# Attention scores of two heads on the two row halves of TensorE, in three float32r passes, with keys and queries split once per pair of heads

## The chip, the cores and the metric

The kernel runs on one core of one Trainium2 chip. The metric is the device time of one execution in microseconds (us): the median of three runs. The profile is of one execution that took 1009.93 us on the device; its span, from the first to the last instruction, is 1008.2 us.

## The reference

Attention over 4 batches and 12 heads, sequence 448, head size 64, with a mixing of heads before and after the softmax ("talking heads"), then a two-layer perceptron:

```python
scores = scale * np.matmul(q, k.transpose(0, 1, 3, 2))          # per head, 448 x 448, scale 1/8
scores = np.einsum('bhij,hg->bgij', scores, w_pre)              # mix heads
scores = scores - np.max(scores, axis=-1, keepdims=True)
attn = np.exp(scores)
attn = attn / (np.sum(attn, axis=-1, keepdims=True) + 1e-09)
attn = np.einsum('bhij,hg->bgij', attn, w_post)                 # mix heads
x = np.matmul(attn, v)                                          # then (b i) x (h d) = 1792 x 768
h = x @ w_in                                                    # 768 x 2048
out = np.maximum(0.01 * h, h) @ w_out                           # 2048 x 768
```

All inputs and the output are float32.

## The kernel before

A *chunk* is 120 rows of the queries of one batch (88 in the last of the four chunks of a batch); there are 16 chunks. A chunk is cut into groups of ten rows: 12 groups (9 in the short chunk), dealt into three supergroups `s`. The main loop runs over chunks `n` and, inside a chunk, over 12 steps `t = 4 s + c`.

In a step of chunk `n` the program writes down, in this order: `softmax` of one group of the next supergroup (one float32 product with the block-diagonal `kpre` on TensorE into bank `psm`, a maximum on VectorE, an exponential on ScalarE; at a supergroup's last group also the reciprocals and the scaled matrix `kp` on VectorE); in steps 0 to 3 `scores` of three heads of chunk `n + 1`; then, one step late, `mix` of column block `c` of the supergroup before (products with `kp` into bank `psa`, copied to `at` or `half`) or, for c = 3, `values` of the chunk before (bank `psx`, copied to `xo`) around the mix; then `regroup`, a DMA that deals the scores `st` of chunk `n + 1` into group tiles `rt`; and in step 6 `prep_q` of chunk `n + 2`.

`mix` of the last column block writes its two 64-partition output halves as two matmuls (120x64 weights), and `values` writes the even and the odd head of a pair into output partitions 0 to 63 and 64 to 127, also as two matmuls (128x64 weights). These are halves of the array by column.

`scores` of one head are two float32r matmuls with all 128 rows: the keys lie in SBUF with their high part (rounded to float32r) in partitions 0 to 63 and their low part (the rest) in partitions 64 to 127; the queries lie twice, once in each half, and come as a low part `qlo` and a high part `qhi`. So the launch code hands over `q` and `k` doubled to 128 partitions. `prep_k` (lines 163 to 168) makes one head's keys: a cast of 128x448 on VectorE (L166) and a subtraction of 64x448 on GpSimd (L167). `prep_q` (lines 178 to 192) makes one chunk's queries in two calls each of a cast of 128x720 on ScalarE (L190) and a subtraction of 128x720 on GpSimd (L191). The banks `pss` are copied to `st` by ScalarE (L218) and, every third head, VectorE (L216).

GpSimd has one more job: two float32 operations of 128x384 (L116, L117), 60 times over the loop, at the end of the conversion of the perceptron's float64 weights (`Narrow`: ScalarE L99 and L100, VectorE L106, L109 and L112, then GpSimd).

Before the loop stands a prologue: the loads of the first chunk's queries and of 12 heads of keys, their split, the scores of chunk 0, the regrouping and four softmax groups. Behind the loop, from 528 us, runs the perceptron: only float32r matmuls of 128x448 in three passes (L368).

What sets the order: all of attention's matmuls are kept in program order on TensorE (`mm`, L153 and L154), and so are the pieces of `Narrow` on their engines. Everything else is ordered by a planner that puts an instruction on its engine's queue as early as its inputs and a free buffer allow in the planner's own timeline; each engine then works through its queue in that order. PSUM has eight banks: 2 `psm`, 2 `psa`, 1 `psx`, 3 `pss`.

## Time and profile before

| | |
|---|---|
| median of three runs | 1010.64 us (1010.62 to 1011.05) |
| profiled execution | 1009.93 us; span 1008.2 us |
| TensorE busy, share of the span | 947.7 us, 94% |
| VectorE busy | 705.8 us, 70% |
| ScalarE busy | 399.9 us, 40% |
| GpSimd busy | 250.9 us, 25% |
| DMA | 170.98 MB, mean 170 GB/s |
| mean granted TensorE clock | 0.981 |

TensorE's busy time is modelled and matmuls are pipelined, so a busy TensorE may still be waiting a little at each matmul; its idle time is more telling. Names in a row are those of the program (`pss` is a scores bank, `qlo` the low part of the queries). PE is TensorE's matmuls, PEld its weight loads, DVE VectorE, ACT ScalarE, POOL GpSimd, SP the engine that issues most DMAs.

### The profile page before, as it was taken

To read this page: it belongs to the slowest core of one execution; us is meant where nothing else is said; L and a number is where in the kernel's file an instruction comes from. 1 tells how busy PE (TensorE), PEld (TensorE's weight loads), DVE (VectorE), ACT (ScalarE), POOL (GpSimd) and SP (SyncE) were. 2 spreads that over 40 slices of the span, in tenths; PEclk is the share of its full clock that TensorE was granted. 3 is DMA by queue.
4 is the path that set the end of the run, shared out by engine and by line. 5 is a ranking of instruction groups with operands and counts; after the bars stand their busy time and mean duration, and the time that the engine had idled before them with its cause. 6 is when DMAs were issued, how large, how long until landed. Compare 5 with 4: busy or idle time off the path is not lost.

```text
span 1008.2 us, 16745 instructions
## 1 busy us (share of the span) xinstructions
PE 947.7 (94%) x6192; PEld 803.9 (80%) x6192; DVE 705.8 (70%) x1248; ACT 399.9 (40%) x891; POOL 250.9 (25%) x213
## 2 busy tenths in 40 slices
PE   4889899998999989999899999999999999999998
PEld 2567678776777767777679999999999999999997
DVE  6588987789787897778785656865557555665553
ACT  4566566565666656666541112311113111211111
POOL 5146743358434574344120001100000000000000
PEclk9999999998999989999989999999999999999999
DMA  5876756856568654686554434553336333353331
GB/s 179 277 214 224 225 188 202 252 211 214 189 205 267 217 175 154 208 259 222 182 164 142 138 109 139 165 166 110 109 110 199 112 104 111 108 164 110 110 94 55
DMA packets 102917, 170.98 MB, mean 170 GB/s; under 512 B 30260, under 2 KB 76852, under 8 KB 102836
## 3 DMA queue, kind: packets, MB, share of 16 engines
q1 hardware_dynamic: 101108, 167.16, 53.0%
q10 hardware_dynamic: 1728, 2.75, 0.7%
q8 instruction: 49, 0.80, 0.3%
q14 instruction: 32, 0.26, 0.1%
HBM read 107.75 MB, written 23.59 MB: 130 GB/s over the span
## 4 chain that ended last, share of the span: by engine, by line
PE 81%; DVE 9%; issue 4%; DMA 2%; ACT 2%; SPq 1%; POOL 0%; DVEq 0%; ACTq 0%; POOLq 0%
PE psh L368 23%; PE pso L368 23%; PE psa L154 12%; PE psm L154 11%; PE psx L154 6%; PE pss L154 6%; DVE kst L166 2%; DVE kp L255 1%; ACT et L242 1%; DVE stat L241 1%; SPq L228 1%; DVE top L109 1%; DVE top L106 1%; DMA rt<-st 1%; DVE at L290 1%
## 5 line engine op out<-in xcount | busy, mean ns | idle before, releaser
L154 PEld LDWEIGHTS psa<-kp,et 120*128 120x128 f32 (+2 forms) x1800 | 175.0, 176 | 67.0 <-issue 48.4
L154 PE MATMUL psm<-rt,kpre 120*120 120x448 f32 x360 | 180.9, 587 | 22.5 <-ACT et L242 18.9
L154 PE MATMUL psa<-kp,et 120*128 120x120 f32 (+2 forms) x1800 | 182.4, 262 | 20.0 <-DVE kp L255 14.3
L361 DVE CAST wh<-wr 128x768 fp32r<-128x768 f32 x128 | 72.9, 570 | 170.1 <-PE psh L368 113.0
L379 ACT ACTIVATE t<-psh 128x448 f32<-128x448 f32 x64 | 35.0, 547 | 312.2 <-PE psh L368 294.5
L242 ACT ACTIVATE et<-psm,stat 120x448 f32<-120x448 f32 x180 | 113.9, 633 | 86.4 <-DVE stat L241 83.5
L368 PE MATMUL psh<-xh,wl 128*128 128x448 f32 x384 | 140.7, 367 | 0.9 <-issue 0.9
L368 PE MATMUL pso<-gl,wh 128*128 128x448 f32 x384 | 140.2, 365 | 0.0
L368 PE MATMUL pso<-gh,wh 128*128 128x448 f32 x384 | 140.2, 365 | 0.0
L368 PE MATMUL psh<-xh,wh 128*128 128x448 f32 x384 | 140.2, 365 | 0.0
L368 PE MATMUL psh<-xl,wh 128*128 128x448 f32 x384 | 140.2, 365 | 0.0
L368 PE MATMUL pso<-gh,wl 128*128 128x448 f32 x384 | 139.1, 365 | 0.0
L241 DVE TENSOR_REDUCE stat<-psm 120x1 f32<-120x448 f32 x180 | 111.3, 618 | 35.1 <-PE psm L154 32.1
L362 DVE TENSOR_TENSOR wl<-wr,wh 128x768 fp32r<-128x768 f32 x128 | 122.9, 960 | 2.0
L116 POOL TENSOR_TENSOR w<-w,exp 128x384 f32<-128x384 f32 x60 | 62.8, 1046 | 217.0 <-DVE exp L112 91.7
L154 PE MATMUL pss<-kst,qlo 128*120 128x448 f32 (+1 forms) x192 | 94.3, 491 | 12.6 <-POOL kst L167 10.0
L218 ACT ACTIVATE st<-pss 120x448 f32<-120x448 f32 (+1 forms) x132 | 69.3, 543 | 65.4 <-PE pss L154 63.0
L154 PEld LDWEIGHTS psm<-rt,kpre 120*120 120x120 f32 x360 | 54.9, 193 | 36.7 <-ACT et L242 26.1
L368 PEld LDWEIGHTS psh<-xh,wl 128*128 128x128 f32 x384 | 72.1, 188 | 7.1 <-issue 1.0
L290 DVE COPY at<-psa 128x480 f32<-128x480 f32 (+2 forms) x112 | 68.6, 613 | 13.1 <-PE psa L154 11.8
L368 PEld LDWEIGHTS pso<-gh,wh 128*128 128x128 f32 x384 | 72.2, 188 | 5.7
L368 PEld LDWEIGHTS pso<-gl,wh 128*128 128x128 f32 x384 | 72.1, 188 | 5.7
(59 smaller groups left out, 1345.8 us busy)
## 6 DMA issues: line engine op xcount, KB each, us to landing
wr<-w_dram SPq DMA_DIRECT2D x126, 384.0 KB
rt<-st SPq DMA_DIRECT2D x176, 210.0 KB
craw<-in_w_moe SPq DMA_DIRECT2D x64, 384.0 KB
w_dram<-w SPq DMA_DIRECT2D x60, 192.0 KB
kraw<-in_k SPq DMA_DIRECT2D x48, 224.0 KB
qraw<-in_q SPq DMA_DIRECT2D x11, 720.0 KB
xr<-x_dram SPq DMA_DIRECT2D x24, 224.0 KB
vt<-in_v SPq DMA_DIRECT2D x12, 384.0 KB
```

The costliest lines, as they stand in the source:

```text
L106: pin(nc.vector.tensor_scalar(top, z.bitcast(U32), 3, 0x7FFFFFF8, op0=ALU.logical_shift_left, op1=ALU.bitwise_and))
L116: pin(nc.gpsimd.tensor_mul(w, w, self.exp.bitcast(F32)))
L154: tc.keep_in_program_order(nc.tensor.matmul(*args, **kw))
L166: hi(t, raw)
L218: nc.scalar.activation(s_t[n][:m, h, :], ps[:m, :S], AF.Copy, scale=scale)
L241: nc.vector.tensor_reduce(st[:kk, 0, g:g + 1], ps[:kk, :S], axis=AX.X, op=ALU.max, negate=True)
L242: nc.scalar.activation(e[:kk], ps[:kk, :S], AF.Exp, bias=st[:kk, 0, g:g + 1], accum_out=st[:kk, 1, g:g + 1])
L290: copy(at[:, :, i:i + full * ROWS].rearrange("p h (g r) -> p g h r", r=ROWS), ps[:, :w * full].rearrange("p (g h r) -> p g h r", h=nh, r=R ...
L361: nc.vector.tensor_copy(hi, raw)
L362: nc.vector.tensor_sub(lo, raw, hi.bitcast(F32))
L368: nc.tensor.matmul(ps, w[a][:, c * P:(c + 1) * P], x[e], start=first and j == 0, stop=last and j == 2)
L379: nc.scalar.activation(t, ps[:, :S], AF.Copy, scale=0.01)
```

## The change

Keys and queries are no longer doubled in SBUF: partitions 0 to 63 hold the even head of a pair, partitions 64 to 127 the odd one. (The launch code is as before; the loads take the half that they need.) `prep_k` splits a pair at once into a high tile and a low tile of 128x448, the subtraction on VectorE. `prep_q` splits six pairs in two calls of 128x360 (three pairs each), cast on ScalarE, subtraction on VectorE. GpSimd does neither any more.

`scores(n, j)` does two pairs (four heads): per pair three passes (low queries with high keys, high with low, high with high), each pass two matmuls with 64 rows, one per head, on the two row halves and into two banks. The product of the two low parts is dropped. Four banks are filled: two `pss` and two `psx` (now two of these, and two `pss` in place of three). Three of the four are copied by ScalarE, one by VectorE.

The three calls of a chunk stand in steps 2, 6 and 10, and two of them lie a chunk earlier than before: in step 2 of chunk `n` the last third of chunk `n + 1`, in steps 6 and 10 the first two thirds of chunk `n + 2`. So `st` has two buffers, `prep_q` moves to step 3, the load of queries to step 6 and one chunk ahead, and `regroup` runs from step 4 to 8 (before from 3 to 7). Keys of the next batch are loaded and split every second step over some 17 steps. The prologue does the first two thirds of chunk 1's scores as well.

```diff
@@ -141,54 +141,58 @@
     pool = pools(psum, "left")
     ps_m = pool("ps_m", 2, space=PSUM)
     ps_a = pool("ps_a", 2, space=PSUM)
-    ps_x = pool("ps_x", 1, space=PSUM)
+    ps_x = pool("ps_x", 2, space=PSUM)
     pool = pools(right, "right")
     p_raw = pool("raw", 1)
     p_q = pool("q", 1)
-    p_k = pool("k", H + 2)
-    p_s = pool("s", 1)
+    p_k = pool("k", NPAIR)
+    p_s = pool("s", 2)
     p_c = pool("c", 1)
-    ps_s = pool("ps_s", 3, space=PSUM)
+    ps_s = pool("ps_s", 2, space=PSUM)
 
     def mm(*args, **kw):
         tc.keep_in_program_order(nc.tensor.matmul(*args, **kw))
 
     kw_t, k_t, q_t, v_t, s_t, r_t, e_t, kp_t, at_t, xo_t = ({} for _ in range(10))
 
-    def load_k(b, h):
+    def load_k(b, a):
         t = p_raw.tile([P, S], F32, tag="k", name="kraw", bufs=6)
-        kw_t[b, h] = t
-        return nc.sync.dma_start(t, k[b, :, h, :])
-
-    def prep_k(b, h, hi=nc.vector.tensor_copy, lo=nc.gpsimd.tensor_sub):
-        raw = kw_t.pop((b, h))
-        t = p_k.tile([P, S], F32R, tag="k", name="kst")
-        hi(t, raw)
-        lo(t[D:], raw[D:], t[D:].bitcast(F32))
-        k_t[b, h] = t
-
-    def load_q(n, *heads):
+        kw_t[b, a] = t
+        for e in range(2):
+            up = slice(D * e, D * (e + 1))
+            nc.sync.dma_start(t[up], k[b, up, 2 * a + e, :])
+
+    def prep_k(b, a, hi_op=nc.vector.tensor_copy):
+        raw = kw_t.pop((b, a))
+        hi = p_k.tile([P, S], F32R, tag="khi", name="khi")
+        lo = p_k.tile([P, S], F32R, tag="klo", name="klo")
+        hi_op(hi, raw)
+        nc.vector.tensor_sub(lo, raw, hi.bitcast(F32))
+        k_t[b, a] = hi, lo
+
+    def load_q(n):
         b, i0, m, _ = chunks[n]
-        if n not in kw_t:
-            kw_t[n] = p_raw.tile([P, H, CHUNK], F32, tag="q", name="qraw")
-        src = q[b, :, H * i0:H * (i0 + m)].rearrange("p (h i) -> p h i", h=H)
-        for a, z in heads or ((0, H),):
-            nc.sync.dma_start(kw_t[n][:, a:z, :m], src[:, a:z])
-
-    def prep_q(n, hi_op=nc.scalar.copy, lo_op=nc.gpsimd.tensor_sub):
+        kw_t[n] = p_raw.tile([P, NPAIR, CHUNK], F32, tag="q", name="qraw")
+        src = q[b, :, H * i0:H * (i0 + m)].rearrange("p (a e i) -> p a e i", e=2, i=m)
+        for e in range(2):
+            up = slice(D * e, D * (e + 1))
+            nc.sync.dma_start(kw_t[n][up, :, :m], src[up, :, e])
+
+    def prep_q(n, *hi_op):
         m = chunks[n][2]
         raw = kw_t.pop(n)
         if m % ROWS:
             nc.gpsimd.memset(raw[:, :, m:-(-m // ROWS) * ROWS], 0.0)
         m = -(-m // ROWS) * ROWS
-        hi = p_q.tile([P, H, CHUNK], F32R, tag="qhi", name="qhi")
-        lo = p_q.tile([P, H, CHUNK], F32R, tag="qlo", name="qlo")
-        for a in (0, H // 2):
-            at = slice(a, a + H // 2)
+        hi = p_q.tile([P, NPAIR, CHUNK], F32R, tag="qhi", name="qhi")
+        lo = p_q.tile([P, NPAIR, CHUNK], F32R, tag="qlo", name="qlo")
+        half = NPAIR // 2
+        for i, op in enumerate(hi_op or (nc.scalar.copy, nc.scalar.copy)):
+            at = slice(half * i, half * (i + 1))
             dealt = raw[:, at, :m].rearrange("p h (g r) -> p h r g", r=ROWS)
             to_hi, to_lo = (t[:, at, :m].rearrange("p h (r g) -> p h r g", r=ROWS) for t in (hi, lo))
-            hi_op(to_hi, dealt)
-            lo_op(to_lo, dealt, to_hi.bitcast(F32))
+            op(to_hi, dealt)
+            nc.vector.tensor_sub(to_lo, dealt, to_hi.bitcast(F32))
         q_t[n] = hi, lo
 
     v_end = p_v.tile([P, NPAIR, 2, D], F32, tag="end", name="vend")
@@ -203,19 +207,26 @@
             nc.sync.dma_start(v_end[up, RUN * s:RUN * (s + 1), e], v[b][up, NJ - 1, at + e:at + 2 * RUN:2])
         v_t[b, s] = t
 
-    def scores(n, h):
+    def scores(n, j):
         b, i0, m, _ = chunks[n]
         m = -(-m // ROWS) * ROWS
-        if h == 0:
+        if j == 0:
             s_t[n] = p_s.tile([CHUNK, H, S], F32, tag="s", name="st")
-        hi, lo = q_t[n]
-        ps = ps_s.tile([CHUNK, 512], F32, tag="s", name="pss")
-        for i, w in enumerate((lo, hi)):
-            mm(ps[:m, :S], w[:, h, :m], k_t[b, h], start=i == 0, stop=i == 1)
-        if n and h % 3 == 2:
-            nc.vector.tensor_scalar_mul(s_t[n][:m, h, :], ps[:m, :S], scale)
-        else:
-            nc.scalar.activation(s_t[n][:m, h, :], ps[:m, :S], AF.Copy, scale=scale)
+        (qh, ql), banks = q_t[n], []
+        for a, pool, tag in ((RUN * j, ps_s, "s"), (RUN * j + 1, ps_x, "x")):
+            kh, kl = k_t[b, a]
+            two = [pool.tile([P, 512], F32, tag=tag, name="pss") for _ in range(2)]
+            for i, (x, y) in enumerate(((ql, kh), (qh, kl), (qh, kh))):
+                for e in range(2):
+                    up = slice(D * e, D * (e + 1))
+                    mm(two[e][:m, :S], x[up, a, :m], y[up], start=i == 0, stop=i == 2)
+            banks += two
+        for e, ps in enumerate(banks):
+            to = s_t[n][:m, 2 * RUN * j + e, :]
+            if e == 2:
+                nc.vector.tensor_scalar_mul(to, ps[:m, :S], scale)
+            else:
+                nc.scalar.activation(to, ps[:m, :S], AF.Copy, scale=scale)
 
     last_dma = [None]
 
@@ -300,7 +311,7 @@
         at, half = at_t[n]
         if s == 0:
             xo_t[n] = p_x.tile([P, NPAIR, CHUNK], F32, tag="xo", name="xo")
-        ps = ps_x.tile([P, 4, P], F32, tag="x", name="psx")
+        ps = ps_x.tile([P, 512], F32, tag="x", name="psx").rearrange("p (a i) -> p a i", a=4)
         w = v_t[b, s]
         for a in range(RUN):
             mm(
@@ -395,18 +406,18 @@
                 (nc.scalar, nc.sync)[c % 2].dma_start(out[c * P:(c + 1) * P, b * S:(b + 1) * S], o)
 
 
-    load_q(0, (0, H // 2))
-    for h in range(3):
-        load_k(0, h)
-    load_q(0, (H // 2, H))
-    prep_q(0, nc.vector.tensor_copy, nc.vector.tensor_sub)
-    for h in range(H + 1):
-        if h < H:
-            prep_k(0, h, (nc.vector.tensor_copy, nc.scalar.copy)[h % 2], (nc.gpsimd.tensor_sub, nc.vector.tensor_sub)[h % 2])
-        if h + 3 < H:
-            behind = load_k(0, h + 3)
-        if h:
-            scores(0, h - 1)
+    for a in range(RUN):
+        load_k(0, a)
+        if a == 0:
+            load_q(0)
+    prep_q(0, nc.vector.tensor_copy, nc.scalar.copy)
+    for a in range(NPAIR):
+        prep_k(0, a, nc.scalar.copy)
+        if a + RUN < NPAIR:
+            load_k(0, a + RUN)
+        if a % RUN:
+            scores(0, a // RUN)
+    load_q(1)
 
     wt = const.tile([RH, 2, H], F32, name="wt")
     for i, w in enumerate((w_pre, w_post)):
@@ -425,14 +436,14 @@
             compare_op=ALU.is_ge, fill=0.0,
         )
 
-    with tc.issue_after(behind.ins):
-        load_q(1)
-
     regroup(0, 0, SLOTS)
     ctx.enter_context(tc.issue_after(last_dma[0].ins))
     for s in range(3):
         load_v(0, s)
-    prep_q(1, nc.vector.tensor_copy)
+    prep_q(1)
+    for j in range(2):
+        scores(1, j)
+    load_q(2)
     for g in range(NJ):
         softmax(0, 0, g)
 
@@ -457,8 +468,8 @@
             s, c = divmod(t, NJ)
             last = n == NCK - 1
 
-            if t == 0 and n + 2 < NCK:
-                load_q(n + 2)
+            if t == HALF and n + 3 < NCK:
+                load_q(n + 3)
             step_no = n * SLOTS + t
             due = step_no // EVERY
             if step_no % EVERY == 1 and due - 1 in narrowing:
@@ -470,30 +481,29 @@
             if step_no % EVERY == 0 and pieces and not last:
                 with tc.issue_after(last_dma[0].ins):
                     narrowing[due] = Narrow(p_c, *pieces.pop(0))
-            if n % NB == NB - 2 and b + 1 < B:
-                load_k(b + 1, t)
-            if n % NB == NB - 1 and b + 1 < B and t < 2:
-                prep_k(b + 1, H - 2 + t)
+            due = (n % NB - 1) * SLOTS + t - 3
+            if b + 1 < B and due % 2 == 0:
+                if 0 <= due < 2 * NPAIR:
+                    load_k(b + 1, due // 2)
+                if 0 <= due - 2 * NPAIR // 2 < 2 * NPAIR:
+                    prep_k(b + 1, (due - NPAIR) // 2)
 
             nxt = (n, s + 1) if s < 2 else (n + 1, 0)
             if nxt[0] < NCK and c < len(chunks[nxt[0]][3][nxt[1]]):
                 softmax(*nxt, c)
-            if t < NJ and not last:
-                for h in range(3):
-                    scores(n + 1, 3 * t + h)
+            if c == 2 and n + 1 + (s > 0) < NCK:
+                scores(n + 1 + (s > 0), (s + 2) % 3)
             if late:
                 step(*late)
             late = n, s, c
 
-            if not last and NJ - 1 <= t < 2 * NJ:
-                a = 2 * (t - NJ + 1) + 2 * (t >= NJ)
-                regroup(n + 1, a, 2 * (t - NJ + 3))
-            if t == HALF and n + 2 < NCK:
+            if not last and NJ <= t <= 2 * NJ:
+                a = 2 * (t - NJ) + 2 * (t > NJ)
+                regroup(n + 1, a, 2 * (t - NJ) + 4)
+            if t == 3 and n + 2 < NCK:
                 prep_q(n + 2)
             if n > 1 and t == 0:
                 store_x(n - 2)
-            if n % NB == NB - 2 and b + 1 < B and t > 1:
-                prep_k(b + 1, t - 2)
             if last and t < NC:
                 load_x(0, t)
             if last and 1 < t < NC + 2:
```

## Rows read from the trace of the kernel before

**Rows 1.** Stretches: span, then busy us (instructions) of PE, PEld, DVE, ACT, POOL; clock; DMA.

```profile
0.00:25.52 25.52, 11.06 (x24) 6.48 (x25) 15.95 (x20) 10.58 (x19) 13.88 (x16) 1.00 0.55 179
25.52:528.48 502.96, 461.47 (x3734) 357.52 (x3735) 405.46 (x800) 300.15 (x708) 227.06 (x190) 0.96 0.65 212
554.98:1008.20 453.22, 448.70 (x2215) 415.56 (x2213) 269.25 (x401) 85.47 (x156) 9.99 (x8) 1.00 0.42 123
```

**Rows 2.** Page, chain of waits: share of the span by engine.

```profile
PE 81%; DVE 9%; issue 4%; DMA 2%; ACT 2%; SPq 1%; POOL 0%; DVEq 0%; ACTq 0%; POOLq 0%
```

**Rows 3.** PE's waits, 60 to 547 us: total us, times, longest.

```profile
PE psm L154 <- ACT et L242: 15.4, 13, 2.5
PE psa L154 <- DVE kp L255: 14.3, 4, 3.9
PE psa L154 <- DVE at L290: 5.7, 3, 1.9
```

**Rows 4.** POOL in order of time: two of the 15 runs of the queries' low part.

```profile
174.85 4.23 POOL L191 TENSOR_TENSOR qlo<-qraw,qhi 128x720 fp32r<-128x720 f32 x2 [2.87 <-ACT qhi L190]
...
459.54 3.31 POOL L191 TENSOR_TENSOR qlo<-qraw,qhi 128x540 fp32r<-128x540 f32 x2 [2.55 <-ACT qhi L190]
```

**Rows 5.** DVE in order of time, beside the first of those two runs.

```profile
175.58 1.57 DVE L106 TENSOR_SCALAR top<-z 128x384 uint32<-128x384 uint32 x1
177.19 2.31 DVE L109 SCALAR_TENSOR_TENSOR top<-z,top 128x384 uint32<-128x384 uint32 x1
```

**Rows 6.** Groups by shape, 0 to 520 us: busy us, mean ns, idle before.

```profile
L191 POOL TENSOR_TENSOR qlo<-qraw,qhi 128x720 fp32r<-128x720 f32 x22 | 47.7, 2192 | 35.5 <-ACT qhi L190 32.4 <-DVE qhi L190 2.9
L191 DVE TENSOR_TENSOR qlo<-qraw,qhi 128x720 fp32r<-128x720 f32 x2 | 3.6, 1823 | 0.1
L166 DVE CAST kst<-kraw 128x448 fp32r<-128x448 f32 x42 | 29.2, 715 | 0.2
L345 DVE TENSOR_TENSOR xl<-xr,xh 128x448 fp32r<-128x448 f32 x10 | 6.9, 695 | 3.8 <-ACT xh L344 3.7
L109 DVE SCALAR_TENSOR_TENSOR top<-z,top 128x384 uint32<-128x384 uint32 x60 | 52.8, 881 | 0.8
L190 ACT CAST qhi<-qraw 128x720 fp32r<-128x720 f32 x20 | 28.9, 1503 | 0.0
L218 ACT ACTIVATE st<-pss 120x448 f32<-120x448 f32 x100 | 52.7, 544 | 48.7 <-PE pss L154 46.3 <-DMA vt<-in_v 2.3
L154 PEld LDWEIGHTS psx<-at,vt 128*64 128x64 f32 x1032 | 51.3, 139 | 0.0
L154 PEld LDWEIGHTS psx<-half,vend 128*128 128x128 f32 x172 | 26.4, 194 | 12.4 <-issue 11.4 <-DMA rt<-st 0.4
```

**Rows 7.** PE in order of time behind that run, and at the last chunk.

```profile
181.23 1.25 PE L154 MATMUL psm<-rt,kpre 120*120 120x448 f32 x2 [2.48 <-ACT et L242]
182.27 1.90 PE L154 MATMUL psa<-kp,et 120*128 120x120 f32 x8
...
504.44 2.03 PE L154 MATMUL psa<-kp,et 120*128 120x120 f32 x8 [3.91 <-DVE kp L255]
```

**Rows 8.** PE in order of time: start, duration in us, line, output and inputs, count.

```profile
323.44 0.71 PE L154 MATMUL pss<-kst,qlo 128*120 128x448 f32 x1
323.99 0.36 PE L154 MATMUL pss<-kst,qhi 128*120 128x448 f32 x1
...
324.99 1.05 PE L154 MATMUL psa<-kp,et 120*128 120x120 f32 x8
325.88 0.92 PE L154 MATMUL psm<-rt,kpre 120*120 120x448 f32 x2
...
333.39 1.41 PE L154 MATMUL psx<-at,vt 128*64 128x120 f32 x24
```

**Rows 9.** The stretch behind the first run of rows 4; columns as in rows 1.

```profile
180.00:185.00 5.00, 3.77 (x12) 2.78 (x13) 2.81 (x7) 3.08 (x9) 2.05 (x3) 0.69 0.74 252
```

**Rows 10.** PE in order of time: its first product behind chunk 0's scores.

```profile
25.52 6.48 PE L154 MATMUL psm<-rt,kpre 120*120 120x448 f32 x8 [3.44 <-DMA rt<-st]
```

## The prediction

> **What bounds the kernel now.** I read the stretches first. The perceptron (from 555 us) keeps TensorE busy for 448.7 of 453.2 us [rows 1]; the change does not touch it, so everything is decided before. In the attention loop, 25.5 to 528.5 us, TensorE is busy 461.5 of 503.0 us, VectorE 405.5, ScalarE 300, GpSimd 227, and the granted clock is 0.96 on average, not 1.00 [rows 1]. So TensorE is the bound, with 41.5 us of idle time and some 20 us (4% of 503) lost to the lower clock. The chain says the same from the end: TensorE 81%, VectorE next with 9% [rows 2].
>
> Next, whom TensorE waits for. From 60 to 547 us three kinds of wait hold nearly all: the exponential (15.4 us), `kp` (14.3) and the `at` copy (5.7), 35.4 us together [rows 3]. These are results of ScalarE and VectorE, so I asked what delays those two. In order of time nearly every long wait comes just behind a run of two subtractions on GpSimd, the queries' low part, 15 in all, one per chunk [rows 4]. Beside the run at 174.85 us two VectorE operations take 1.57 and 2.31 us [rows 5], where the second kind takes 0.88 on average with the held ones in it [rows 6]; they end where the GpSimd operations end. Behind it TensorE runs dry for 2.48 us, and then eight `psa` matmuls last 1.90 us [rows 7] where eight normally start a new group after 0.89 (324.99 to 325.88) [rows 8]: TensorE has fallen to its lower level, 1.2 GHz. That stretch of 5 us has a mean clock of 0.69 [rows 9], which costs 1.55 us on top of the wait.
>
> **The change part by part.** All sums are against the profiled execution, 1009.93 us with a span of 1008.2 us; the 1.7 us around the span stay. The median of three runs is 0.7 us above that execution, less than anything below.
>
> *Scores on TensorE.* Six matmuls of three heads take 1.55 us from the first start to what follows, but the first one still waits for the product before it; the other five are 0.20 apart [rows 8]. I count 6 x 0.20 + 0.1 = 1.3 us a block. In the loop there are 15 chunks x 4 blocks = 60, or 78 us. Afterwards a block has 12 matmuls of 64 rows in six pairs. If the two of a pair run side by side, a pair takes 0.20; if in turn, 0.41. No row shows row halves. The nearest shows column halves: 24 matmuls of 120 columns into the two output halves end after 1.41 us, 59 ns each, while the full ones take 111 ns (eight in 0.89) [rows 8], so two halves pass in about the time of one. I take side by side. The weight loads need a look too: one of 64 columns takes 139 ns, one of 128 takes 194 [rows 6], 0.86 ns a column, so 120 columns occupy 0.10 us and the two loads of a pair, in turn, 0.21. That just fits. With 0.15 us for entering the other layout, a block takes 6 x 0.21 + 0.15 = 1.4 us. Of 48 blocks five lie in the prologue, 43 in the loop: 60 us, so 18 us less. Bounds: 20 us less (0.20 a pair and 0.1 for entering) to 34 us more (0.41 a pair: 43 x 2.6 = 112).
>
> That row halves run at once is also what the Trainium skill says (TensorE: Matmul & The Clock Gate, Part 3: matmuls on distinct row groups run concurrently); by it the pair takes 0.20. The same section says that a weight load overlaps a running matmul only when the row groups differ. The trace does not agree for whole-array loads, where five matmuls that each bring their own weights follow at 0.20 [rows 8]; by the rule the next load for a half would wait for the matmul on that half, and the result is the third rival below.
>
> *Queries' split.* The two GpSimd subtractions of a chunk (2.19 us each [rows 6]) go. Of the 35.4 us of waits I leave out the one at 504.44 us (3.9 [rows 7], from the last chunk, where `kp` is late for another reason) and about 3.5 us of waits of 1 us and less elsewhere: 28 us are theirs. Of the 20 us of lost clock I give them 9, six stretches like that of [rows 9]. In place of it VectorE gets two subtractions of half the size, 0.91 us each by the 1.82 of the two that VectorE does now [rows 6] (0.56 by the 0.695 of a contiguous 128x448, 1.1 at most), and ScalarE two casts of about 0.75 instead of 1.50 [rows 6]. That holds VectorE for 1.8 us a chunk instead of 4.2. TensorE ran dry by about 2 us behind a hold of about 4, so it carries about 2 us of work in hand; a hold of 1.8 costs little. I take 0.3 us for each of 15, so 28 - 4 = 24 us less, and 9 less from the clock. Bounds: 0 (everything behind the new subtractions is just as late) to 37.
>
> *Keys' split.* VectorE: 12 casts of 0.715 a batch, 8.6 us, become 6 casts and 6 subtractions of 0.695, 8.5 us [rows 6]: nothing. GpSimd's part goes. I take 1 us less, bounds 0 to 4 less (the short waits above).
>
> *Copies out of the banks.* ScalarE copies nine banks a chunk instead of eight, three in a row (1.63 us at 0.544 [rows 6]) where two stood before (1.09). The exponential of that step is queued behind them, and TensorE waits for it. The 2 us in hand cover 0.54 more; without that cover it is 43 x 0.54 = 23 us. I take 5 us more, bounds 0 to 23. The second pair's banks are shared with `values`; two steps (a step is 503 / 192 = 2.6 us) lie between them either way, against 1.6 us of copies, so I cost that wait at nothing.
>
> *Moves.* The loads of keys are as many as before at half the size, those of queries two instead of one, each a quarter of the bytes, so SP issues 16 more DMAs and moves half as much. `regroup` starts a step later and loses 2.6 us of four to five steps' lead, but the copies that it waits for are two steps old by then. None of TensorE's named waits is one for a DMA [rows 3]. Nothing, bounds 0 to 5 more.
>
> *Prologue.* Now TensorE idles 3.44 us for chunk 0's regrouping and starts its first product at 25.52 us [rows 10]. Afterwards all six pairs of keys find a buffer at once, GpSimd's subtractions are gone, and two blocks of chunk 1 fill the wait, though they need chunk 1's queries split first. I take 3 us less, bounds 8 less to 3 more.
>
> Sum: 1008.2 - 18 - 24 - 9 - 1 + 5 - 3 = 958.2, and 1.7 around it: **960 us**.
>
> **Rivals.** *VectorE takes over.* Its 405 us in the loop become about 405 + 25 (28 subtractions of 0.91) - 32 (15 runs, at least 2.1 us of holding each: 3.9 less twice 0.88) - 9 (one score copy fewer a chunk) = 389, in a loop of 453 instead of 503 us: 86% instead of 81%. For it: VectorE's results are what TensorE waits for already. Against it: those waits come in bursts behind GpSimd. If VectorE keeps the 97 us of idle time that it has now, the loop takes 486: about 990 us.
>
> *The halves run in turn* (the other side). A pair takes 0.41, a block 2.6 instead of 1.4: 48 x 1.2 = 58 more, **1018 us**, slower than before although GpSimd's holds are gone. It decides from 0.38 us a pair on (50 us more / 288 pairs = 0.17 above 0.21). For it: no row shows row halves, nor any float32r matmul in halves. Against it: the column halves.
>
> *Weight loads in turn with the matmuls of their half.* Then a pair takes 0.20 + 0.10 = 0.31: 288 x 0.10 = 29 more, 989 us. Against it: the spacing of 0.20 with full weights.
>
> **How the numbers follow.** Forecast 0.60 (945 to 975), VectorE 0.15 (975 to 995), weight loads 0.10 (975 to 1000), in turn 0.12 (1003 to 1025), better than 945 0.03. The range 945 to 1002 leaves out the last two. About 0.2% (2 us) is what a measurement here can tell from no change. Faster by more than that: 0.87, all but the in-turn case, which may land just below; within it 0.03; slower 0.10.
>
> **What would show it.** Right: two `pss` matmuls start within some ns of each other and a block lasts about 1.4 us; no VectorE operation of 2 us and no TensorE wait over 1 us once a chunk; the loop's clock at 0.98 or more; the first perceptron matmul near 478 instead of 528 us. Wrong: matmuls of a block 0.20 apart, twelve in 2.5 us; VectorE above 95% in the loop with waits for `kp` or the exponential behind its new subtractions; waits behind the three copies on ScalarE.

## The result, and the profile after

The kernel after takes **974.68 us** (median of 4 runs, 972.91 to 983.12) against 1010.63 us for the kernel before on the same chip: a ratio of 0.9666, 95% interval 0.9608 to 0.9725. Ratios, here and below, leave out executions more than 1.5% above the fastest of their kernel, so they can differ from the ratio of the medians. The profiled execution took 974.31 us; its span is 972.6 us, so 35.6 us less than before.

The same three stretches as in [rows 1], here cut at the first softmax product and just behind the start of the first `pso` matmul of the perceptron (columns: span, then busy us and instructions of PE, PEld, DVE, ACT, POOL, then granted clock, DMA share, GB/s):

```profile
0.00:24.83 24.83, 13.58 (x60) 9.97 (x60) 10.25 (x18) 13.83 (x24) 2.29 (x9) 1.00 0.47 138
24.83:518.26 493.43, 468.48 (x4106) 344.59 (x4106) 390.68 (x840) 289.58 (x727) 125.98 (x124) 0.98 0.67 205
518.26:972.60 454.34, 449.92 (x2221) 416.57 (x2219) 269.31 (x401) 85.10 (x155) 10.00 (x8) 1.00 0.41 122
```

The kernel before, for the stretch from its first softmax product to its first `pso`:

```profile
25.52:554.98 529.46, 487.97 (x3955) 381.85 (x3956) 420.63 (x827) 303.83 (x716) 227.06 (x190) 0.96 0.65 209
```

The perceptron takes 454.34 us where it took 453.22 [rows 1], and the first softmax product comes 0.7 us earlier. So the whole difference, 529.46 - 493.43 = 36.0 us, is in the attention loop. TensorE's idle time in it falls from 41.5 to 25.0 us, the granted clock rises from 0.96 to 0.98.

One thing has to be known before totals are compared. The perceptron is the same code in every run below, and yet its matmuls follow at 0.203 us in some profiled executions and at 0.207 in others. 100 us of it in which TensorE is busy throughout at a clock of 1.00, first after, then `after_whole_rows` (a run below):

```profile
600.00:700.00 100.00, 100.00 (x495) 92.67 (x494) 62.66 (x93) 20.16 (x37) 1.63 (x2) 1.00 0.48 142
```

```profile
600.00:700.00 100.00, 100.00 (x485) 90.83 (x485) 61.18 (x90) 19.22 (x35) 1.74 (x2) 1.00 0.46 140
```

From the first `pso` to the end of the span that makes 454 or 463 us, a difference of 9 us in code that the edits of the attention loop do not touch. The times of some kernels fall into two groups as far apart (`after_two_edits`: 971.7 twice, 979.7 to 981.5 four times); that this is the same effect is likely, but only one execution of each kernel was profiled. So below each run also has the start of its first `pso`, which stands ahead of the effect: 518.1 us in after, 554.8 in the kernel before.

What answers to [rows 3], TensorE's waits from 60 to 520 us (total us, times, longest):

```profile
PE psm L154 <- ACT et L253: 7.1, 5, 5.3
PE psa L154 <- DVE kp L266: 3.7, 8, 0.6
PE psa L154 <- DVE at L301: 2.4, 1, 2.4
PE psx L154 <- DVE st L227: 1.5, 3, 0.5
PE psh L379 <- DVE wl L373: 1.1, 1, 1.1
PE psa L154 <- ACT at L301: 0.9, 3, 0.3
```

Together 16.7 us, and 7.7 of them are two waits in the last chunk (5.3 and 2.4); in the chunks between, nothing is over 1 us. The block of two pairs, with what stands around it (PE in order of time: start, duration, line, output and inputs, count):

```profile
307.95 0.92 PE L154 MATMUL psm<-rt,kpre 120*120 120x448 f32 x2
308.80 0.44 PE L154 MATMUL pss<-khi,qlo 64*90 64x448 f32 x2
309.07 0.36 PE L154 MATMUL pss<-klo,qhi 64*90 64x448 f32 x2
309.28 0.37 PE L154 MATMUL pss<-khi,qhi 64*90 64x448 f32 x2
...
309.89 0.36 PE L154 MATMUL pss<-khi,qhi 64*90 64x448 f32 x2
310.18 1.15 PE L154 MATMUL psa<-kp,et 120*128 120x120 f32 x8
311.17 0.92 PE L154 MATMUL psm<-rt,kpre 120*120 120x448 f32 x2
311.92 1.05 PE L154 MATMUL psa<-kp,et 120*128 120x120 f32 x8
```

Two matmuls of a pair start as one group, and the pairs are 0.20 us apart: the row halves run side by side. The block costs more than six slots (a slot is the 0.20 us from one matmul of 448 columns to the next), though. From the `psm` before it to the `psa` behind it are 310.18 - 307.95 = 2.23 us; without a block that is 311.92 - 311.17 = 0.75; and the `psa` behind the block holds TensorE for 0.99 (311.17 - 310.18) where one takes 0.89 [rows 8]. So a block is 2.23 - 0.75 + 0.10 = 1.58 us: 1.22 for the pairs and 0.36 for going into the half layout and out of it. A block of the kernel before, six matmuls over all rows, costs 1.22 us by the same reckoning: from the `psm` at 325.88 [rows 8] to the `psa` behind the block 1.97 us, less 0.75, and that `psa` holds TensorE for 0.88 as without a block (kernel before, PE in order of time):

```profile
327.85 1.05 PE L154 MATMUL psa<-kp,et 120*128 120x120 f32 x8
328.73 0.92 PE L154 MATMUL psm<-rt,kpre 120*120 120x448 f32 x2
```

What answers to [rows 6] on VectorE, from 60 to 460 us (busy us, mean ns; idle time before):

```profile
L109 DVE SCALAR_TENSOR_TENSOR top<-z,top 128x384 uint32<-128x384 uint32 x55 | 30.4, 553 | 0.9
L195 DVE TENSOR_TENSOR qlo<-qraw,qhi 128x360 fp32r<-128x360 f32 (+1 forms) x26 | 19.6, 782 | 2.1 <-ACT qhi L194 2.1
```

The 2.31 us operation of [rows 5] is gone (0.553 on average against 0.88), and the queries' subtraction costs 0.78 us a call, 1.6 a chunk.

### The profile page after: what moved, and what is told of

Same layout as the page of the kernel before. It is cut to its first block, busy times and chain, and to the rows that moved or that the text cites. A ratio compares the mean times of both kernels' runs of the same rounds, so it can differ in the third digit from the quotient of the medians.

```text
span 972.6 us, 17036 instructions
## 1 busy us (share of the span) xinstructions
PE 932.0 (96%) x6384; PEld 771.1 (79%) x6384; DVE 670.2 (69%) x1257; ACT 388.5 (40%) x906; POOL 138.3 (14%) x141
## 4 chain that ended last, share of the span: by engine, by line
PE 80%; DVE 8%; DMA 5%; ACT 3%; SPq 2%; issue 2%; ACTq 0%; DVEq 0%
PE pso L379 24%; PE psh L379 23%; PE psa L154 12%; PE psm L154 10%; PE psx L154 6%; PE pss L154 5%; DMA w_dram<-w 3%; DVE stat L252 1%; DMA rt<-st 1%; SPq L239 1%; DVE qlo L195 1%; ACT st L229 1%; DVE kp L266 1%; DVE wl L373 1%; DVE at L301 1%
## 5 line engine op out<-in xcount | busy, mean ns | idle before, releaser
L154 PEld LDWEIGHTS psa<-kp,et 120*128 120x128 f32 (+2 forms) x1800 | 162.5, 171 | 69.3 <-issue 43.9
L154 PE MATMUL psa<-kp,et 120*128 120x120 f32 (+2 forms) x1800 | 179.3, 260 | 10.3 <-DVE kp L266 6.7
L154 PE MATMUL psm<-rt,kpre 120*120 120x448 f32 x360 | 172.8, 564 | 12.0 <-ACT et L253 12.0
L379 PEld LDWEIGHTS psh<-xl,wh 128*128 128x128 f32 x384 | 72.2, 188 | 5.9 <-issue 0.2
L379 PEld LDWEIGHTS psh<-xh,wh 128*128 128x128 f32 x384 | 72.1, 188 | 5.7
L379 PEld LDWEIGHTS pso<-gh,wl 128*128 128x128 f32 x384 | 72.1, 188 | 5.7
```

The lines of the kernel that those rows point to most:

```text
L154: tc.keep_in_program_order(nc.tensor.matmul(*args, **kw))
L379: nc.tensor.matmul(ps, w[a][:, c * P:(c + 1) * P], x[e], start=first and j == 0, stop=last and j == 2)
```

## The experiments

A ratio is to the kernel before, run in the same session; after stands at 0.9666. In the diffs only what differs is shown.

**Who subtracts.** The prediction put the waits down to GpSimd's subtractions. Two runs take them off GpSimd in the kernel before, one puts them back in after.

`before_q_vec`:

```diff
-    def prep_q(n, hi_op=nc.scalar.copy, lo_op=nc.gpsimd.tensor_sub):
+    def prep_q(n, hi_op=nc.scalar.copy, lo_op=nc.vector.tensor_sub):
```

> The kernel before with only the queries' low part on VectorE; the keys' low part stays on GpSimd. Theory 1 with the queries' two long operations as the cause: 985 us, within 6 us of the run that moves both. Rival (the keys' 42 operations of 1.27 us count as much): halfway between 1010 and the run that moves both. Rival 1: 1005 to 1015.

`before_split_vec` does the same in `prep_k` too (`lo=nc.vector.tensor_sub`).

> The kernel before with both low parts (queries and keys) subtracted on VectorE instead of GpSimd, the scores as they were. Theory 1 (about two thirds of the gain is that GpSimd no longer holds VectorE, one third the row halves): 980 us, 972 to 990; the waits of 1 to 4 us once a chunk and the stretches at the lower clock behind them are gone. Rival 1 (the row halves brought nearly all, the holds only filled time that TensorE did not need): 1005 to 1015. Rival 2 (the row halves brought nothing, what they save goes into entering and leaving the other layout): 972 to 978, the time of the changed kernel.

`after_split_pool`:

```diff
-            nc.vector.tensor_sub(to_lo, dealt, to_hi.bitcast(F32))
+            nc.gpsimd.tensor_sub(to_lo, dealt, to_hi.bitcast(F32))
...
-        nc.vector.tensor_sub(lo, raw, hi.bitcast(F32))
+        nc.gpsimd.tensor_sub(lo, raw, hi.bitcast(F32))
```

> The changed kernel with both low parts back on GpSimd (128x360 and 128x448 a time), the scores on the row halves and their places as in the changed kernel. Theory 1: 995 us, 988 to 1005: VectorE operations of 1.1 to 2.2 us beside GpSimd and waits of TensorE behind them. Rival 1: 973 to 980, as the changed kernel. Rival 2: 1010, as the kernel before.

Measured: 1010.45 us (ratio 1.0012, 0.9991 to 1.0034), 1022.26 (1.011, 1.007 to 1.015) and 977.27 (0.968, 0.9644 to 0.9715). The first theory missed in all three, by 25, 42 and 18 us. Rival 1 has the numbers of the first and the third, but its reason, the row halves, does not hold (below). Taking the subtraction off GpSimd gains nothing (with the keys' too it loses 11 us), and giving it back costs nothing; `after_split_pool` also has its first `pso` at 518.0 us, like after. Why the first two gain nothing is seen in TensorE's waits of `before_q_vec`, 60 to 547 us:

```profile
PE psa L154 <- DVE kp L255: 21.4, 4, 6.8
PE psm L154 <- ACT et L242: 14.3, 14, 2.2
PE psa L154 <- DVE at L290: 4.3, 3, 1.5
```

The sum, 40.0 us, is no smaller than the 35.4 of [rows 3]. The waits for `kp` grow from 14.3 to 21.4 us; there are four of them in either kernel, all at a change of batch or in the last chunk. In `before_split_vec`, the kernel's VectorE queue shows how (in order of time, at a change of batch):

```profile
244.19 1.42 DVE L191 TENSOR_TENSOR qlo<-qraw,qhi 128x720 fp32r<-128x720 f32 x1
...
246.09 1.54 DVE L191 TENSOR_TENSOR qlo<-qraw,qhi 128x720 fp32r<-128x720 f32 x1
...
248.19 0.72 DVE L167 TENSOR_TENSOR kst<-kraw,kst 64x448 fp32r<-64x448 f32 x1
...
252.86 0.65 DVE L255 TENSOR_TENSOR kp<-kpost,stat 120x480 f32<-120x480 f32 x1
253.66 2.03 PE L154 MATMUL psa<-kp,et 120*128 120x120 f32 x8 [8.92 <-DVE kp L255]
```

Between its first queries' subtraction and `kp` VectorE works without a pause; TensorE stands still for 8.92 us and then runs eight matmuls in 2.03 us, at its lower level.

**What the row halves are worth on TensorE.** `after_in_turn` writes the six matmuls of the lower half first, then the six of the upper half:

```diff
+        for e in range(2):
+            for h, a in enumerate((RUN * j, RUN * j + 1)):
+                kh, kl = k_t[b, a]
+                for i, (x, y) in enumerate(((ql, kh), (qh, kl), (qh, kh))):
+                    up = slice(D * e, D * (e + 1))
+                    mm(banks[2 * h + e][:m, :S], x[up, a, :m], y[up], start=i == 0, stop=i == 2)
```

> The changed kernel with the twelve matmuls of a block ordered by row half: six on the lower half, then six on the upper half, so that only at the middle two can run side by side (11 slots of 0.20 us instead of 6). Theory 1 (TensorE is the bound and the halves run side by side): a block takes 2.4 to 2.6 us instead of 1.4, 45 blocks and more, so 40 to 48 us more: 1015 to 1022 us. Rival 2 (the halves do not shorten the loop): 973 to 985.

Measured: 998.82 us (0.9891, 0.9864 to 0.9918), 24.1 us above after's 974.68, about half of what was expected. Its PE in order of time says why:

```profile
316.76 0.44 PE L154 MATMUL pss<-khi,qlo 64*90 64x448 f32 x1
...
317.24 0.36 PE L154 MATMUL pss<-khi,qhi 64*90 64x448 f32 x1
317.25 0.56 PE L154 MATMUL pss<-khi,qlo 64*90 64x448 f32 x2
...
318.34 0.36 PE L154 MATMUL pss<-khi,qhi 64*90 64x448 f32 x1
318.63 1.15 PE L154 MATMUL psa<-kp,et 120*128 120x120 f32 x8
```

The row at 317.25 joins two matmuls that start 0.20 us apart (0.56 is 0.36 + 0.20). One starts together with the lower half's third, at 317.24; matmuls of one half follow 0.20 apart, so it must be the upper half's first, and the other is the lower half's fourth. From there the two halves run beside each other, although the program writes the upper half's six behind the lower half's six, and the last matmul starts at 318.34. The block goes from 1.38 (310.18 - 308.80) to 1.87 us (318.63 - 316.76), 2.4 slots more in place of five. Over the 43 blocks in the loop 0.49 us makes 21 us. The first `pso` is at 532.4 us, 14.3 later than in after; TensorE's idle time in the loop is 21.3 us in place of 25.0, so a part comes back in shorter waits. So TensorE's time in the blocks counts for two thirds; the other 9 us of the total are the perceptron's (463.3 us).

`after_whole_rows` keeps after's order, splits and copies and gives TensorE eight whole-array matmuls a block in place of six pairs (a product is left out and two heads are added up, so the output is not the reference's):

```diff
-            for i, (x, y) in enumerate(((ql, kh), (qh, kl), (qh, kh))):
-                for e in range(2):
-                    up = slice(D * e, D * (e + 1))
-                    mm(two[e][:m, :S], x[up, a, :m], y[up], start=i == 0, stop=i == 2)
+            for e in range(2):
+                for i, x in enumerate((ql, qh)):
+                    mm(two[e][:m, :S], x[:, a, :m], kh, start=i == 0, stop=i == 1)
```

> The kernel after with its order of the work, its copies and its splits, but each head's scores in two matmuls over all 128 rows (low and high part of the queries, each against the high part of both heads' keys) in place of three over 64 rows beside the other head's. The score of a head is then the sum of two heads and a product is left out, so the output is not the reference's; TensorE's work is that of the kernel before: eight matmuls in a row a block in place of six pairs. Theory (the even spacing removed the waits, the row halves are worth only what is left of two fewer slots a block after the switch of layout): two more slots of 0.20 us less a switch of about 0.26 us in each of 48 blocks, +7 us, about 981 us. Rival (the halves carry the gain, as the prediction's scores term of 18 us has it): 992 us or more. Second rival (a switch of layout costs 0.1 to 0.15 us): +0.25 us in 48 blocks, 987 us.

Measured: 981.92 us, ratio 0.97 (0.9663 to 0.9737); 0.0034 above after's ratio, 3.4 us, and the intervals overlap. The first theory's 981 is met by luck: the profiled execution is 7.5 us longer than after's, but its perceptron takes 463.3 us, and its first `pso` comes at 516.7 us, 1.4 before after's. The block, PE in order of time:

```profile
305.93 0.92 PE L154 MATMUL psm<-rt,kpre 120*120 120x448 f32 x2
306.33 0.72 PE L154 MATMUL pss<-khi,qlo 128*90 128x448 f32 x1
...
308.32 1.05 PE L154 MATMUL psa<-kp,et 120*128 120x120 f32 x8
```

From `psm` to `psa` 2.39 us, less the 0.75: 1.64 us for eight slots with no change of layout, against 1.58 in after. The two slots that the halves save (0.41 us) go almost wholly into the change of layout (0.36). That would be 43 x 0.06 = 2.6 us; the loops of the two profiled executions differ by 0.6.

`after_split_blocks` cuts each block into two of one pair, so that the layout changes twice as often:

```diff
-            if c == 2 and n + 1 + (s > 0) < NCK:
-                scores(n + 1 + (s > 0), (s + 2) % 3)
+            if 0 < c < 3 and n + 1 + (s > 0) < NCK:
+                scores(n + 1 + (s > 0), (s + 2) % 3, (c - 1,))
```

> The kernel after with each block of two pairs (twelve matmuls) cut into two blocks of one pair (six matmuls) in two steps that follow each other; every matmul, copy and split stays. That adds one more change between the whole array and its halves, there and back, for each of the 45 blocks within the loop. Theory (a change there and back costs about 0.36 us, by the edges of a block in the trace of after): +16 us, about 991 us. Rival (0.10 to 0.15 us, what the prediction took for it): +5 to +7 us, 980 us. Rival (a finer spacing helps ScalarE and VectorE more than the switch costs): 975 us or less.

Measured: 986.09 us (0.9741, 0.971 to 0.9771), 7.6 us more than after by the ratios. The profiled execution is 12.8 us longer, but 9 of them are the perceptron's (463.4 us): the first `pso` comes at 522.1 us, 4.0 later than in after. The total lies between the first two expectations, the loop below both. In its trace a block of one pair costs 0.97 us by the same reckoning (`psm` at 310.99, `psa` at 312.61: 1.62 - 0.75 + 0.10), two of them 1.94, which is 0.36 more than one block of two pairs, as the first theory has it. Over the 43 blocks that are cut that would be 15 us; more than half of it comes back, since TensorE's idle time in the loop is 16.5 us in place of 25.0.

**What the even spacing is worth.** `after_bunched` keeps every matmul, split and copy of after and puts the three blocks into steps 1 to 3:

```diff
-            if c == 2 and n + 1 + (s > 0) < NCK:
-                scores(n + 1 + (s > 0), (s + 2) % 3)
+            if 0 < t < 4 and n + 1 < NCK:
+                scores(n + 1, t - 1)
...
-            due = (n % NB - 1) * SLOTS + t - 3
+            due = (n % NB - 1) * SLOTS + t - 9
```

> The kernel after with the three score blocks of a chunk in three steps that follow each other (steps 1 to 3 of the chunk before) and no blocks of chunk 1 ahead of the first softmax; the keys' splits six steps later, so that they still stand behind the last block that reads the old keys. Theory (even spacing is what removed the waits): VectorE and ScalarE get twelve score copies, the queries' split and a part of the keys' splits within some 15 us of each chunk again, and TensorE's waits of the kernel before for kp and et (about 33 us in the loop) come back for the most part: 990 to 1003 us. Rival (row halves and fewer matmuls carry the gain, the spacing nothing): 975 to 979 us.

Measured: 1019.17 us, median of ten runs from 1004.56 to 1025.76; ratio 1.0031 (0.9997 to 1.0065). The whole gain is gone: the first `pso` comes at 557.8 us (perceptron 462.2). TensorE's waits of the profiled execution, which is one of the longer ones (1021.71 us), 60 to 520 us:

```profile
PE psm L154 <- ACT et L253: 17.3, 9, 3.6
PE pss L154 <- ACT st L229: 10.5, 4, 4.5
PE psx L154 <- ACT st L229: 5.2, 3, 1.8
```

All three, the largest, are ScalarE. In its queue (in order of time, ACT and PE):

```profile
187.08 0.55 ACT L99 ACTIVATE z<-craw 128x384 f32<-128x384 f32 x1 [4.83 <-DMA craw<-in_w_moe]
...
187.96 0.62 ACT L253 ACTIVATE et<-psm,stat 120x448 f32<-120x448 f32 x1
...
188.57 1.40 ACT L229 ACTIVATE st<-pss 120x448 f32<-120x448 f32 x3
189.16 0.90 PE L154 MATMUL pss<-khi,qlo 64*120 64x448 f32 x2 [3.12 <-ACT st L229]
```

ScalarE waits 4.83 us for a load of weights, and behind that conversion stand an exponential and three copies, without which the next block finds no bank. From 60 to 520 us ScalarE waits 27.6 us in 10 places for these loads; in after 2.3 us in 2. Why they come later when the blocks are bunched was not settled.

`after_two_apart` is the step between: blocks in steps 11, 1 and 3.

```diff
+            if t in (1, 3, 11) and n + 1 + (t > 3) < NCK:
+                scores(n + 1 + (t > 3), {11: 0, 1: 1, 3: 2}[t])
```

> The kernel after with the three blocks of a chunk two steps apart (steps 11, 1 and 3) in place of four, the keys three steps later, one block of chunk 1 ahead of the first softmax in place of two. Theory (what costs is score copies that meet in ScalarE and VectorE and matmuls that wait for a block's banks; with two steps between them the banks are free again, but the copies still meet the queries' split at step 3): 980 to 995 us. Rival (only blocks in steps that follow each other cost, the rest is free): 973 to 978 us.

Measured: 1013.17 us, ratio 0.9988 (0.995 to 1.0026). Both expectations missed: by the total, two steps between blocks are as bad as none. In the profiled execution (1003.04 us, perceptron 453.4) the first `pso` comes at 548.0 us, 6.8 before the kernel before and 29.9 behind after, so most of the gain is gone here as well. The copies do not need to meet; ScalarE waits 13.2 us in 9 places for the loads of weights here too, and TensorE 17.7 us for exponentials.

`after_keys_bunched` leaves the blocks in place and puts the six pairs of key splits of a batch into six steps in a row.

```diff
+            at = (n % NB - 2) * SLOTS + t - 3
+            if b + 1 < B and 0 <= at < NPAIR:
+                prep_k(b + 1, at)
```

> The kernel after with the six pairs' key splits in six steps in a row (steps 3 to 8 of the third chunk of each batch, where the queries' split is too) in place of every second step over two chunks. Score blocks keep their places. Theory (spacing of the score blocks is what matters; keys' splits are six times 1.2 us of VectorE a batch): 975 to 981 us. Rival (the pile of keys' splits made the long waits of the kernel before at the change of batch): 10 us or more, 985 us.

Measured: 978.07 us, ratio 0.9667 (0.9619 to 0.9715). The theory holds; in the profiled execution the first `pso` comes at 515.0 us, even 3.1 before after's (perceptron 463.5). Of the even spacing, that of the score blocks counts.

**The even spacing alone.** `before_even` is the kernel before with its own arithmetic and splits, in after's order:

```diff
-            if t < NJ and not last:
-                for h in range(3):
-                    scores(n + 1, 3 * t + h)
+            if c == 2 and n + 1 + (s > 0) < NCK:
+                for h in range(4):
+                    scores(n + 1 + (s > 0), (s + 2) % 3 * 4 + h)
...
-    p_s = pool("s", 1)
+    p_s = pool("s", 2)
```

> The kernel before with its own arithmetic (keys' low part under the high one, queries on both row halves, two matmuls a head over all 128 rows, low parts on GpSimd, the larger reads of keys and queries) and the order of the kernel after: four heads' scores in steps 2, 6 and 10, a chunk earlier, one head's keys a step, a second buffer of scores, two banks for the values' products in place of one, shared with the scores. Nothing of the row halves and of the smaller splits is in it. Theory (the even spacing is nearly the whole gain, the row halves are worth about 7 us): 978 to 986 us. Rival (spacing pays only with the smaller splits: GpSimd and ScalarE still split twice the queries): 995 us or more.

Measured: 1008.86 us, ratio 0.9973 (0.9941 to 1.0005). The theory missed by over 20 us, and the rival holds: spacing without the smaller splits is worth at most some us. In the profiled execution the loop up to the first `pso` is 6.9 us shorter than in the kernel before, but the first softmax product comes 6.2 us later (31.7 us), behind the two blocks of chunk 1 and their large split. Its waits, 60 to 547 us, and its VectorE beside the key splits (order of time):

```profile
PE psa L154 <- DVE kp L255: 22.7, 18, 1.9
PE psm L154 <- ACT et L242: 5.5, 4, 3.5
```

```profile
99.22 2.38 POOL L167 TENSOR_TENSOR kst<-kraw,kst 64x448 fp32r<-64x448 f32 x2 [1.18 <-issue]
...
100.53 1.62 DVE L166 CAST kst<-kraw 128x448 fp32r<-128x448 f32 x2
```

The exponentials are no longer late (5.5 us against 15.4), but `kp` is, 18 times, and most of that time (13.5 us) in the stretches in which keys are split. There VectorE does less in the same time than in after. The stretch from 75 to 125 us, first `before_even`, then after:

```profile
75.00:125.00 50.00, 44.04 (x357) 33.33 (x357) 45.65 (x80) 30.07 (x71) 32.31 (x26) 1.00 0.72 227
```

```profile
75.00:125.00 50.00, 48.72 (x442) 35.88 (x441) 43.85 (x98) 30.20 (x77) 12.93 (x12) 1.00 0.73 221
```

80 instructions in 45.65 us against 98 in 43.85, beside a GpSimd that is busy for 32.31 us against 12.93. Operations of one shape take longer: the casts of the keys, of which there are also twice as many, in that stretch, `before_even`, then after (busy us, mean ns; idle time before):

```profile
L166 DVE CAST kst<-kraw 128x448 fp32r<-128x448 f32 x12 | 8.7, 754 | 0.0
```

```profile
L169 DVE CAST khi<-kraw 128x448 fp32r<-128x448 f32 x6 | 2.6, 433 | 0.2 <-PE pss L154 0.2
```

The larger loads of the kernel before are in this run too, but VectorE waits only 0.7 us for keys from 60 to 460 us.

**Two attempts at something faster.** After's trace shows two waits left at its ends, both of them ScalarE casts that wait for a DMA with an exponential behind. `after_two_edits` loads chunk 2's queries ahead of the first values and splits the perceptron's rows of batch 0 on GpSimd:

```diff
+    load_q(2)
     for s in range(3):
         load_v(0, s)
...
-        nc.scalar.copy(hi, raw)
-        nc.vector.tensor_sub(lo, raw, hi.bitcast(F32))
+        (nc.scalar.copy if b else nc.gpsimd.tensor_copy)(hi, raw)
+        (nc.vector if b else nc.gpsimd).tensor_sub(lo, raw, hi.bitcast(F32))
```

> The kernel after with two edits where its trace shows waits that the change put there or left: the load of chunk 2's queries ahead of the loads of the first values (ScalarE's cast of these queries waited 2.5 us for it, with the first exponentials of chunk 0 behind it), and the split of batch 0's rows for the perceptron on GpSimd in place of ScalarE and VectorE (ScalarE's cast waited 6.1 us for its transfer in the last chunk, with an exponential behind it that TensorE then waited 5.3 us for). Theory (in-order queues make these waits; both waits are on the path): 3 to 4 us less at the start and 4 to 6 at the end, with TensorE's clock not falling behind them 1 to 4 more: 962 to 968 us. Rival (the next release, a DMA of the first values or VectorE's keys' output, is late instead): 971 to 975 us.

Measured: 979.95 us, ratio 0.9679 (0.9647 to 0.9712): no gain in the total, so the rival's reading, some us above its number. The profiled execution (971.72 us, perceptron 453.5) has its first `pso` at 516.5 us, 1.6 before after's, where 7 us or more were expected. The wait for the exponential in the last chunk is gone, and the next release is late in its place (PE in order of time):

```profile
465.02 0.71 PE L379 MATMUL psh<-xh,wl 128*128 128x448 f32 x1 [6.47 <-POOL xl L356]
```

`after_later_blocks` puts chunk 1's blocks into steps 1 to 3 of chunk 0, with the earlier load of queries:

```diff
+            if not n and 0 < t < 4:
+                scores(1, t - 1)
-            if c == 2 and n + 1 + (s > 0) < NCK:
+            if c == 2 and (n or s) and n + 1 + (s > 0) < NCK:
```

> The kernel after with chunk 1's three score blocks in steps 1 to 3 of chunk 0 in place of two of them ahead of the first softmax, and chunk 2's queries loaded ahead of the first values; from step 6 on everything as in after. Theory (the two blocks stand in front of chunk 0's work, which begins at 24.83 us in after and at 20.05 in the bunched one; chunk 1 begins there at 47.8 us, in after at 56.4): 4 to 8 us less, 966 to 971 us. Rival (the start is bound by the reads of values and keys, and what is gained there is waited for in chunk 1 or 2): 973 to 977 us.

Measured: 978.71 us, ratio 0.9651 (0.9602 to 0.9701), not to be told from after. Counting softmax products (24 a chunk), chunk 1 begins 8.7 us earlier (47.3 against 56.0 us) and chunk 2 still 4.4 earlier (79.6 against 84.0): half is given back in chunk 1, with the clock at 0.91 from 47 to 83 us. The rest stays: the first `pso` comes at 513.5 us, 4.6 before after's, which is what the theory has. Then the perceptron of this execution takes 463.3 us and hides it. So no version here beats after in its total by more than can be measured, but this one is ahead of it when the perceptron starts, in the one execution profiled.

## Why the prediction was right, and where it was wrong

The forecast of 960 us was 15 us too low, the direction and the range right. Term by term, on the spans:

| term | predicted | seen |
|---|---|---|
| scores on TensorE | -18 | -5.3 |
| waits (queries' split -24, keys -1, copies +5) | -20 | -18.7 |
| clock | -9 | -10.2 |
| prologue, to the first product | -3 | -0.7 |
| perceptron | 0 | +1.1 |
| sum | -50 | -33.8 (measured -35.6) |

*Scores on TensorE: the term that was mis-sized.* Side by side at 0.20 a pair was right, and with it the rejection of the two rivals that priced a pair at 0.31 and 0.41. The 0.15 us for the other layout was not: 0.36 by the edges of a block, and by `after_split_blocks` again. So 43 blocks in the loop take 43 x 1.58 = 68 us, not 60. The 1.3 us for a block of the kernel before was too much as well: 1.22 by its edges, so 60 blocks take 73 us, not 78, and what is left of the 18 us is 73.2 - 67.9 = 5.3. `after_whole_rows` takes it apart. A chunk's scores go from 4 x 1.22 = 4.88 us to 3 x 1.64 = 4.92 with whole rows, so fewer and longer blocks gain nothing; the halves make it 3 x 1.58 = 4.74 (15 x 0.18 = 2.7 us, which the totals cannot tell from nothing); and two blocks of chunk 1 have gone into the prologue (2 x 1.58 = 3.2). So the row halves, the name of the change, are among its smallest parts. The term's lower bound has a slip too: 43 x 1.3 = 56 us is 22 less than 78, not 20.

*Queries' split: the size came out right by luck, since the reason was wrong.* The prediction tied 28 us of waits and 9 of clock to GpSimd's subtractions, by the operations held beside them [rows 4, 5], and gave the spacing no term. The waits did fall from 35.4 to 16.7 us, and the stretches at the lower level from 37.4 to 17.0 us of half clock (from the clock of 99 stretches of 5 us; half of it is lost time, 18.7 and 8.5). But `before_q_vec` and `before_split_vec` take the subtractions off GpSimd and gain nothing, and `after_split_pool` puts them back and loses nothing. What the runs show in place of it is two conditions that are worth little without each other: splits of half the size (`before_even` has the spacing without them: 0.9973) and score blocks four steps apart and a chunk early (`after_bunched` and `after_two_apart` have the small splits without it: 1.0031 and 0.9988). The second is shown, since these two runs change little else. The first is argued in part: `before_even` differs from after in more than the size of the splits, its large splits also stand beside a busier GpSimd, and large splits wholly on VectorE were not run with spaced blocks. With only one of the two TensorE's waits stay large and change their name (idle in the loop 44.7, 48.1 and 38.9 us in these three runs, 41.5 in the kernel before, 25.0 in after): `kp` on VectorE where the splits are large, exponentials and score copies on ScalarE where the blocks are close. The step from "the waits stand behind the GpSimd runs" to "they go when these go" was the wrong one: it did not ask what else was queued on VectorE in the same steps. The prediction's first rival, VectorE taking over, is in fact what `before_split_vec` does; in after it did not come, since VectorE does 98 instructions from 75 to 125 us without TensorE waiting over 1 us for it.

*Copies and moves.* The 5 us for a third copy on ScalarE cannot be seen in after: TensorE waits 1.5 us for `st` in all. That `regroup` and the queries' load move was costed at nothing; TensorE's waits name no DMA in after, though one cast of queries waits for its load in chunk 0 (below), and `after_bunched` shows that the order of these moves is not free: ScalarE's waits for the loads of weights rise from 2.3 to 27.6 us.

*Prologue.* Two blocks of chunk 1 fill the wait for the regrouping as expected, but the first product comes at 24.83 us, for chunk 1's queries are late (PE, order of time):

```profile
19.77 0.73 PE L154 MATMUL pss<-khi,qlo 64*120 64x448 f32 x2 [2.17 <-DVE qlo L195]
...
24.83 2.22 PE L154 MATMUL psm<-rt,kpre 120*120 120x448 f32 x4
```

Behind it, chunk 0 and the last chunk hold nearly all that is left to gain, each with one ScalarE cast that waits for a transfer (3.47 and 5.30 us on PE) and a spell at the lower level after it:

```profile
43.92 1.85 PE L154 MATMUL psm<-rt,kpre 120*120 120x448 f32 x2 [3.47 <-ACT et L253]
...
461.13 1.85 PE L154 MATMUL psm<-rt,kpre 120*120 120x448 f32 x2 [5.30 <-ACT et L253]
```

The prediction also took 2 us for what a measurement here can tell; the four executions of after lie 10 us apart, and 9 us can come from the perceptron alone.

What stays open: 1.8 us between the sum of the terms and the span; what sets the perceptron's spacing; why the loads of weights land late for ScalarE when blocks are closer than four steps; and whether smaller splits would gain in the kernel before with its own order of blocks, which was not run (`after_bunched` has four banks for scores in three steps, the kernel before three in four).

## What to carry to other kernels

When TensorE waits behind a busy neighbour, list everything that the engine it waits for has queued in those steps; moving one piece to another engine only renames the wait. Spreading pieces of work evenly and shrinking them can each be worth a few us alone and 36 us together, so test them together before dropping either. Two matmuls on the row halves cost one slot, but going into that layout and out of it costs about two: put many pairs into one block, or expect little over whole-array matmuls, even where those need four slots for three. And where a long stretch of unchanged code follows, compare executions at its start and not only at the end: here 9 us came and went behind it.

## What the runs showed of the hardware that was not expected

A change of layout, there and back, took 0.36 us on TensorE, as much as 1.8 matmuls of 448 columns at 0.20 us. The same matmuls of the perceptron, at a granted clock of 1.00, followed at 0.203 us in some executions and 0.207 in others; no run here shows why. And in `after_in_turn` the seventh matmul of a block, the first on the upper row half, started beside the third (317.25 and 317.24 us), ahead of the fourth, fifth and sixth on the lower half (0.20 apart): order between the halves was not kept there, and the overlap halved the cost of writing them in turn. The Trainium skill (TensorE: Matmul & The Clock Gate, Part 3: Packing small matmuls, The mechanism) says that matmuls start and end in program order without reordering; if these records are matched to the right instructions and TensorE's queue holds them as the program writes them, this trace does not agree.
